# Chunked attention into a bilinear feed-forward: sums and scores in shared runs from block 4 on, and a last product in two column halves

## The chip, the cores and the metric

The kernel runs on one core of a Trainium2 chip. The metric is the device time of one execution in microseconds (us). The engines are TensorE (PE in the profile; PEld is its weight load), VectorE (DVE), ScalarE (ACT), GpSimd (POOL) and SyncE (SP), which here only issues DMAs.

## The reference

```
scores = q_c @ k_c^T / 8           # chunks of 64 tokens, 8 heads, head dim 64
attn   = exp(scores - max) / (sum + 1e-9)
x      = attn @ v                  # laid out as 4608 tokens x 512
out    = ((x @ w_a) * (x @ w_b)) @ w_out   # d_ff 1536, float32
```

The batch has 8 sequences of 576 tokens, so 4608 tokens in all.

## The kernel before

**Units and blocks.** Tokens go in 18 units of 256 (attention) and 9 blocks of 512 (feed-forward): block K uses units 2K and 2K+1. For a unit U there are these steps: `scores` (q times k in 64x64 tiles of TensorE, into two PSUM banks, then two exponentials on ScalarE into `E`), `sums` (E times a matrix of ones, also on 64x64 tiles, into two banks; two Ln on ScalarE, L305), `inverse` (exp of minus Ln, L314), and `values` (E times v on 64x64 tiles, then two multiplies on VectorE, L337, that write `xT`). Scores issued with `now=1` run the first exponential at once and keep the second in a list `late`, which `exps()` empties after `p5`.

**Loads.** `bring(U)` casts the unit's raw q and k on GpSimd (L213), loads unit U+1 on SP (L182), transposes q and k by DMA on SP (L248) and casts v.

**The feed-forward.** From block 2 on, d_ff goes in six groups of 256 (i = 0 to 5). Each group forms the two products of x with w_b and w_a by a seven-product scheme over 2x2 quarters: `p1` to `p7`, four matmuls each of 128x128 by 256 columns (L439). They accumulate in three banks: A (pool psum_a, "pa"), B (one of two banks "pb") and C (psum_c, "pc"). ScalarE copies A to B after `p1` (L457), and stages B after `p6` as u, A after `p2` as b, B after `p5` as v (L450). After `p7`, `add7` on VectorE makes c = C + v (L477) and C += u (L478); then `p3` adds to B and `p4` to C, each followed by a multiply into `ab_sb` (L489). Group i's `p3` and `p4` are issued inside group i+1. The buffers u, b, v, c have one copy each. GpSimd forms the sums of quarters of `ab_sb` (L519).

**The output.** `OutGroup(K-1)` does block K-1's product with w_out during block K, again with seven parts n = 0 to 6 in two halves th = 0, 1 of six matmuls (L575). Parts 0 and 1 go into A (psum_o, "po"), parts 2, 3 and 5 into B (psum_q, "pq"), parts 4 and 6 into C (psum_o again). After part 1 ScalarE writes half of o0 (L590); after 2 and 3 it stages u and v (L595, L598); after 5 it writes the rest of o0 (L602) and SP stores it. After part 4 VectorE writes half of o1 (L618) and does C += u (L622); after part 6 it writes the rest (L608) and SP stores it. At the very end, block 8's own output runs as two `OutGroup`s of one half each (`only` = 0, 1), on 256-column tiles.

**The order is written out by hand.** Each engine runs its instructions in the order of the program. `chunk(n)` takes the next n of the waiting halves of output parts; the table `chunks` holds two numbers for each group. `attend(K, i, n)` runs the attention steps that `at(...)` has put at that place. One group runs so:

```
now.p1()                 # and the copy A to B
if last: last.add7()
chunk(first number)
if last: last.p3()
attend(K, i, 0)
now.p6()
if last: last.p4(); finish(last)
now.p2()
chunk(second number)
attend(K, i, 1)
now.p5(); exps()
now.p7()
```

PSUM has eight banks: psum_a, two of psum_b, psum_c, psum_o, psum_q, and two of psum_t ("pt"). From block 2 on, sums and values take their banks from psum_t; scores take psum_o or psum_q, and the free one of psum_b.

Of the kernel before, what the change touches and what calls it, by code (L numbers as in the profile page):

```python
# [16 lines left out]
def kernel(  # L17
# [10 lines left out]
    nc = tc.nc  # L28
# [260 lines left out]

    def sums(U, halves=None):  # L290
        E = E_of[U]
        sm = [bank() for _ in range(2)]
        for cl in range(2):
            for j in range(2):
                nc.tensor.matmul(  # L295
                    sm[cl][j * 64:j * 64 + 64, :],
                    ones[cl * 64:cl * 64 + 64, :],
                    E[cl * 64:cl * 64 + 64, j].rearrange("p m g s -> p (m g s)"),
                    start=True,
                    stop=True,  # L300
                )
        ln_of[U] = sm_pool.tile([128, 2, NKT, 128], FP32, name="ln")
        rs_of[U] = ln_of[U]
        for cl in range(2):
            nc.scalar.activation(  # L305
                out=ln_of[U][:, cl].rearrange("p m n -> p (m n)"), in_=sm[cl], func=AF.Ln
            )
            if halves:
                inverse(U, cl)
# [8 lines left out]
    def values(U):  # L318
# [16 lines left out]
        for cl in range(2):  # L335
            x = x_tiles[K][:, :, 256 * u:256 * u + 256]
            nc.vector.tensor_tensor(  # L337
                out=x.rearrange("p m (g c s) -> p m g c s", g=2, c=2)[:, :, :, cl, :],
                in0=av[cl],
                in1=rs[:, cl].rearrange("p m (g s) -> p m g s", g=2),  # L340
                op=MULT,
            )

# [11 lines left out]

    def bring(U):

        if U >= NU:
            return
        cast(U, "qk")  # L360
        load(U + 1, "q" if U < 9 else "qkv")
        transpose_dma(U)
        bring_v(U)

# [160 lines left out]
    class OutGroup:  # L525
# [20 lines left out]
        def part(self, n, th):  # L546
# [26 lines left out]
            c0 = 0 if one else th * 256  # L573
            for kt in range(HFT):
                nc.tensor.matmul(  # L575
                    t[:, c0:c0 + 256],
                    a[:, kt, th * 128:th * 128 + 128],
                    w[:, kt],
                    start=n in (0, 4) and first and kt == 0,
                    stop=last and kt == HFT - 1,  # L580
                    skip_group_check=True,
                )
            if not last:
                return
# [22 lines left out]
            else:  # L607
# [4 lines left out]
                for c in [th] if one else range(2):  # L612
                    store(
                        self.K, 1, c, self.o1[:, c], lo if one else slice(0, DM),
                        nc.scalar if one and th else nc.sync,
                    )
            if n == (3 if one else 4):
# [35 lines left out]
    with tc.manual_schedule(  # L653
# [178 lines left out]
        def scores_beside(pool):  # L832
            return lambda u: scores(u, (pool, psum_b[0]), 1)

        for K in range(2, NBLK):
            U = 2 * K + 2
            if K == 2:
                at(K, 0, 0, lambda u: combine_x(2, (2, 3)), U)
                at(K, 0, 0, scores, U)
                at(K, 0, 1, sums, U)  # L840
            else:
                attention[K, 0, 0] = [lambda K=K: combine_x(K, (2,))]
                attention[K, 0, 1] = [lambda K=K: combine_x(K, (3,))]
                at(K, 0, 0, sums, U)
            at(K, 1, 0, inverse, U)
            at(K, 2, 1, values, U)
            at(K, 2, 1, scores_beside(psum_o), U + 1)
            at(K, 3, 0, sums, U + 1)
            at(K, 3, 1, inverse, U + 1)
            at(K, 4, 1, values, U + 1)  # L850
            at(K, 4, 1, scores_beside(psum_q), U + 2)
            at(K, 5, 0, lambda u: combine_x(u // 2, (0,)), U + 1)
            at(K, 5, 1, lambda u: combine_x(u // 2, (1,)), U + 1)

        def attend(K, i, n):
# [5 lines left out]
            2: (1, 1, 1, 1, 1, 2, 1, 2, 3, 0, 1, 1),  # L861
            4: (1, 1, 1, 1, 2, 1, 1, 2, 2, 0, 1, 1),
            NBLK - 1: (1,) * 12,
        }
# [8 lines left out]
        for K in range(2, NBLK):  # L873
            for i in range(NWP):
# [3 lines left out]
                if i == 1:  # L878
                    bring(2 * K + 4)
                elif i == 3 and K > 2:  # L880
                    bring(2 * K + 5)
                elif i == 3:
                    cast(9, "qk")
                    load(10)
                    transpose_dma(9)
                if i == 0:
                    g = OutGroup(K - 1)
                    outs += [
                        lambda g=g, n=n, th=th: g.part(n, th) for n in range(7) for th in range(2)
                    ]  # L890
                now = Group(K, i)
                now.p1()
                if last:
                    last.add7()
                chunk(chunks.get(K, chunks[4])[2 * i])
                if K == 2 and i == 0:
# [13 lines left out]
                now.p2()  # L910
                chunk(chunks.get(K, chunks[4])[2 * i + 1])
                attend(K, i, 1)
                now.p5()
                exps()
                now.p7()
                last = now
# [47 lines left out]
```

The softmax here doesn't subtract the row's maximum and nothing guards it: scores larger than these inputs give would overflow.

## Time and profile before

| | us |
|---|---|
| median of 11 runs | 303.9 (303.23 to 305.68) |
| the profiled execution | 303.88 |
| its span, first to last instruction | 302.1 |
| PE busy | 292.0 (97%) |
| DVE busy | 209.1 (69%) |
| ACT busy | 196.4 (65%) |
| POOL busy | 192.5 (64%) |

The granted TensorE clock is 1.0 over the span. A block of the steady part takes about 30 us: block 2 starts near 81, block 4 near 141, block 5 near 171, block 6 near 201. In the timeline one line merges instructions of one kind in order of time: its start, its length, the engine, the source line, the output and inputs by name, and the count.

### The profile page before, as it was taken

What the parts mean: (1) busy time and instruction counts of PE and PEld (TensorE: products, weight loads), DVE (VectorE), ACT (ScalarE), POOL (GpSimd) and SP (SyncE); (2) the same over time, 40 slices, a digit from 0 to 9 for tenths busy, and PEclk for the clock granted to TensorE, in tenths of its full rate; (3) what the DMA queues carried; (4) which work ended last, traced back from release to release, by engine and by line L of the source; (5) the groups of instructions that cost most, each with busy time, mean ns of one, the idle gap of its engine ahead of it and who ended that gap; (6) DMA issues with size and microseconds to landing.
All of it is one profiled execution on the core that took longest, in us unless ns stands there. A gap on an engine that the chain in (4) does not pass through costs nothing.

```text
span 302.1 us, 8588 instructions
## 1 busy us (share of the span) xinstructions
PE 292.0 (97%) x3519; PEld 231.6 (77%) x3521; DVE 209.1 (69%) x341; ACT 196.4 (65%) x355; POOL 192.5 (64%) x180
## 2 busy tenths in 40 slices
PE   6699999999999999999999999999999999999995
PEld 2344467866588888888888888888888888888884
DVE  3456576877757696769576967795779667965773
ACT  2743567448387769676867687768776877567532
POOL 0565758997699598908880888088817801790560
PEclk9999999999999999999999999999999999999999
DMA  7999999998999989989959495949731001100025
GB/s 225 304 374 289 282 342 351 239 219 201 202 246 270 183 201 271 229 189 242 213 114 229 148 211 121 224 152 207 112 99 72 2 2 69 72 1 3 2 79 199
DMA packets 140984, 54.29 MB, mean 180 GB/s; under 512 B 117137, under 2 KB 135057, under 8 KB 140945
## 3 DMA queue, kind: packets, MB, share of 16 engines
q1 hardware_dynamic: 140800, 53.62, 71.0%
q8 instruction: 27, 0.44, 0.6%
q10 hardware_dynamic: 144, 0.13, 0.1%
q14 instruction: 13, 0.10, 0.1%
HBM read 37.75 MB, written 9.44 MB: 156 GB/s over the span
## 4 chain that ended last, share of the span: by engine, by line
PE 83%; DMA 5%; SPq 4%; DVE 3%; POOL 1%; ACT 1%; issue 1%; DVEq 0%; ACTq 0%; POOLq 0%
PE pb L439 19%; PE pc L439 12%; PE pa L439 12%; PE po L575 12%; PE pq L575 10%; PE pb L643 3%; DMA st<-in_k_dram 3%; DMA st<-in_moe_w_b_dram 2%; PE po L389 2%; PE pc L389 2%; PE pa L389 2%; PE pq L389 2%; PE pt L295 2%; PE pt L328 2%; SPq L112 2%; SPq L194 1%
## 5 line engine op out<-in xcount | busy, mean ns | idle before, releaser
L519 POOL TENSOR_TENSOR so<-ab_sb 128x512 f16<-128x512 f16 x23 | 27.4, 1191 | 67.1 <-DVE ab_sb L489 67.1
L439 PEld LDWEIGHTS <-t 128*128 128x128 f16 x504 | 48.3, 98 | 8.5 <-issue 1.7
L439 PE MATMUL pb<-s,wa 128*128 128x256 f16 x336 | 50.6, 273 | 0.0
L439 PE MATMUL pa<-xT,wb 128*128 128x256 f16 x336 | 50.4, 273 | 0.0
L477 DVE TENSOR_TENSOR c_sb<-pc,v_sb 128x512 f32<-128x512 f32 x42 | 28.9, 689 | 28.7 <-ACT v_sb L450 28.7
L575 PEld LDWEIGHTS <-ab_sb 128*128 128x128 f16 x384 | 37.6, 98 | 4.7 <-issue 0.4
L439 PEld LDWEIGHTS <-wb 128*128 128x128 f16 x336 | 32.9, 98 | 4.0
L439 PEld LDWEIGHTS <-wa 128*128 128x128 f16 x336 | 31.8, 98 | 4.3 <-issue 0.2
L489 DVE SCALAR_TENSOR_TENSOR ab_sb<-pc,c_sb 128x512 f16<-128x512 f32 x42 | 29.0, 690 | 7.9 <-PE pc L439 6.7
L450 ACT COPY u_sb<-pb 128x512 f32<-128x512 f32 x42 | 24.7, 588 | 14.8 <-PE pb L439 14.7
L489 DVE SCALAR_TENSOR_TENSOR ab_sb<-pb,b_sb 128x512 f16<-128x512 f32 x42 | 29.0, 690 | 6.1 <-PE pb L439 5.2
L457 ACT COPY pb<-pa 128x512 f32<-128x512 f32 x42 | 24.1, 573 | 10.3 <-PE pa L439 10.0
L575 PEld LDWEIGHTS <-so 128*128 128x128 f16 x288 | 28.1, 98 | 3.4
L450 ACT COPY b_sb<-pa 128x512 f32<-128x512 f32 x42 | 25.0, 595 | 7.1 <-PE pa L439 7.1
L478 DVE TENSOR_TENSOR pc<-pc,u_sb 128x512 f32<-128x512 f32 x42 | 28.9, 689 | 0.0
L519 POOL TENSOR_TENSOR so<-so,ab_sb 128x512 f16<-128x512 f16 x23 | 27.0, 1174 | 1.7
L450 ACT COPY v_sb<-pb 128x512 f32<-128x512 f32 x42 | 24.6, 587 | 5.1 <-PE pb L439 4.4
L519 POOL TENSOR_TENSOR ab_sb<-ab_sb 128x512 f16<-128x512 f16 x23 | 26.7, 1162 | 0.0
L519 POOL TENSOR_TENSOR so<-ab_sb,so 128x512 f16<-128x512 f16 x23 | 26.1, 1162 | 0.0
L439 PE MATMUL pc<-xT,t 128*128 128x256 f16 x168 | 25.2, 273 | 0.1
L439 PE MATMUL pb<-s,t 128*128 128x256 f16 x168 | 25.3, 273 | 0.0
L439 PE MATMUL pc<-s,t 128*128 128x256 f16 x168 | 25.2, 273 | 0.0
(129 smaller groups left out, 565.8 us busy)
## 6 DMA issues: line engine op xcount, KB each, us to landing
out_dram<-o_sb SPq DMA_DIRECT2D x34, 256.0 KB, 2.3
st<-in_v_dram SPq DMA_DIRECT2D x32, 256.0 KB, 4.7
st<-in_k_dram SPq DMA_DIRECT2D x25, 256.0 KB, 4.8
st<-in_q_dram SPq DMA_DIRECT2D x23, 256.0 KB, 4.0
st<-in_moe_w_b_dram SPq DMA_DIRECT2D x6, 512.0 KB, 7.3
st<-in_moe_w_a_dram SPq DMA_DIRECT2D x6, 512.0 KB, 7.0
st<-in_moe_w_out_dram SPq DMA_DIRECT2D x6, 512.0 KB, 6.2
st<-in_q_dram SPq DMA_DIRECT2D x4, 512.0 KB, 5.6
```

The costliest lines, as they stand in the source:

```text
L112: nc.sync.dma_start(out=staged[n, i], in_=src[:, i * WCOL:i * WCOL + WCOL].rearrange("(kt r) c -> r kt c", r=128),)
L295: nc.tensor.matmul(sm[cl][j * 64:j * 64 + 64, :], ones[cl * 64:cl * 64 + 64, :], E[cl * 64:cl * 64 + 64, j].rearrange("p m g s -> p (m g s)"),
L389: nc.tensor.matmul(ps[n], w_ab[n, i][:, kt, o:o + 128], xT[:, kt, c0:c1], start=(kt == 0), stop=(kt == NKT - 1),)
L439: nc.tensor.matmul(t[:, h * 256:h * 256 + 256], w[:, kt, h * 128:h * 128 + 128], x[:, kt], start=start and h == 0 and kt == 0, stop=h == 1 ...
L450: nc.scalar.copy(out=t, in_=src)
L457: nc.scalar.copy(out=self.B, in_=self.A)
L477: nc.vector.tensor_tensor(out=self.c, in0=self.C, in1=self.v, op=ADD)
L478: nc.vector.tensor_tensor(out=self.C, in0=self.C, in1=self.u, op=ADD)
L489: nc.vector.scalar_tensor_tensor(out=self.dst[:, :, c0:c0 + 256], in0=t.rearrange("p (h n) -> p h n", h=2), scalar=AB_SCALE, in1=o.rearran ...
L519: (eng or nc.gpsimd).tensor_tensor(out=o, in0=x0, in1=x1, op=op)
L575: nc.tensor.matmul(t[:, c0:c0 + 256], a[:, kt, th * 128:th * 128 + 128], w[:, kt], start=n in (0, 4) and first and kt == 0, stop=last and ...
L643: nc.tensor.matmul(out_ps[K, tg], ab_tiles[K][:, ft, tg * 128:tg * 128 + 128], wo_sb[:, ft], start=(ft == 0), stop=(ft == NFT - 1),)
```

## The change

The last product (part 6 of the second half, at the very end) is done in two column halves of 128, each followed by its own VectorE operation and its own store, the first from SP's queue, the second from ScalarE's. Unit 1's last multiply into `xT` is done in two halves.

From block 4 on, three steps of different units share one run on 64x64 tiles: the values of a unit, the scores of the unit two on, and the sums of the next. The sums take psum_a and either psum_o or psum_q; the scores take psum_c and the free bank of psum_b. One of the two Ln is issued at once, the other waits in a list `late_ln` for the next `p1`. In block 4's first group the sums of unit 10 and the scores of unit 11 share a run. The output parts of blocks 4 to 7 run in the order 0, 1, 2, 3, 5, 4, 6, and `chunks` can hold a third number, for a chunk between `p5` and `p7`. From block 3's end on, the loads, casts and transposes of a unit are issued earlier: q and k of unit 2K+5 at group 1, its v at group 3, unit 2K+6 at group 5.

```diff
--- before.py
+++ after.py
@@ -287,9 +287,11 @@
             late.pop(0)()
             n -= 1
 
-    def sums(U, halves=None):
+    late_ln = []
+
+    def sums(U, halves=None, pools=(None, None)):
         E = E_of[U]
-        sm = [bank() for _ in range(2)]
+        sm = [bank(p) for p in pools]
         for cl in range(2):
             for j in range(2):
                 nc.tensor.matmul(
@@ -301,10 +303,15 @@
                 )
         ln_of[U] = sm_pool.tile([128, 2, NKT, 128], FP32, name="ln")
         rs_of[U] = ln_of[U]
+        ln = ln_of[U]
         for cl in range(2):
-            nc.scalar.activation(
-                out=ln_of[U][:, cl].rearrange("p m n -> p (m n)"), in_=sm[cl], func=AF.Ln
+            late_ln.append(
+                lambda cl=cl: nc.scalar.activation(
+                    out=ln[:, cl].rearrange("p m n -> p (m n)"), in_=sm[cl], func=AF.Ln
+                )
             )
+        for cl in range(1 if pools[0] else 2):
+            late_ln.pop(0)()
             if halves:
                 inverse(U, cl)
 
@@ -334,12 +341,13 @@
                         )
         for cl in range(2):
             x = x_tiles[K][:, :, 256 * u:256 * u + 256]
-            nc.vector.tensor_tensor(
-                out=x.rearrange("p m (g c s) -> p m g c s", g=2, c=2)[:, :, :, cl, :],
-                in0=av[cl],
-                in1=rs[:, cl].rearrange("p m (g s) -> p m g s", g=2),
-                op=MULT,
-            )
+            for m in (slice(0, 2), slice(2, 4)) if (U, cl) == (1, 1) else [slice(0, 4)]:
+                nc.vector.tensor_tensor(
+                    out=x.rearrange("p m (g c s) -> p m g c s", g=2, c=2)[:, m, :, cl, :],
+                    in0=av[cl][:, m],
+                    in1=rs[:, cl, m].rearrange("p m (g s) -> p m g s", g=2),
+                    op=MULT,
+                )
 
     def slot(s=None, f=None):
 
@@ -353,14 +361,15 @@
         if f is not None:
             values(f)
 
-    def bring(U):
+    def bring(U, names="qkv"):
 
         if U >= NU:
             return
         cast(U, "qk")
         load(U + 1, "q" if U < 9 else "qkv")
         transpose_dma(U)
-        bring_v(U)
+        if "v" in names:
+            bring_v(U)
 
     def bring_v(U):
         cast(U, "v")
@@ -571,16 +580,26 @@
                 lambda: (self.C, a22, t4),
             )[n]()
             c0 = 0 if one else th * 256
-            for kt in range(HFT):
-                nc.tensor.matmul(
-                    t[:, c0:c0 + 256],
-                    a[:, kt, th * 128:th * 128 + 128],
-                    w[:, kt],
-                    start=n in (0, 4) and first and kt == 0,
-                    stop=last and kt == HFT - 1,
-                    skip_group_check=True,
-                )
-            if not last:
+            end = n == 6 and one and th == 1
+            for cols in (slice(0, 128), slice(128, 256)) if end else [slice(0, 256)]:
+                for kt in range(HFT):
+                    nc.tensor.matmul(
+                        t[:, c0:c0 + 256][:, cols],
+                        a[:, kt, th * 128:th * 128 + 128],
+                        w[:, kt, cols],
+                        start=n in (0, 4) and first and kt == 0,
+                        stop=last and kt == HFT - 1,
+                        skip_group_check=True,
+                    )
+                if end:
+                    nc.vector.tensor_scalar(
+                        out=rows(self.o1, cols), in0=self.C[:, cols], scalar1=OUT_SCALE,
+                        scalar2=None, op0=MULT,
+                    )
+                    store(
+                        self.K, 1, th, self.o1[:, th], cols, nc.scalar if cols.start else nc.sync
+                    )
+            if not last or end:
                 return
             if n == 0:
                 self.B = self.bank(1)
@@ -610,10 +629,7 @@
                     scalar2=None, op0=MULT,
                 )
                 for c in [th] if one else range(2):
-                    store(
-                        self.K, 1, c, self.o1[:, c], lo if one else slice(0, DM),
-                        nc.scalar if one and th else nc.sync,
-                    )
+                    store(self.K, 1, c, self.o1[:, c], lo if one else slice(0, DM))
             if n == (3 if one else 4):
                 nc.vector.scalar_tensor_tensor(
                     out=rows(self.o1, hi), in0=halves(self.C), scalar=OUT_SCALE,
@@ -832,6 +848,9 @@
         def scores_beside(pool):
             return lambda u: scores(u, (pool, psum_b[0]), 1)
 
+        def sums_beside(pool):
+            return lambda u: sums(u, pools=(psum_a, pool))
+
         for K in range(2, NBLK):
             U = 2 * K + 2
             if K == 2:
@@ -841,14 +860,26 @@
             else:
                 attention[K, 0, 0] = [lambda K=K: combine_x(K, (2,))]
                 attention[K, 0, 1] = [lambda K=K: combine_x(K, (3,))]
-                at(K, 0, 0, sums, U)
-            at(K, 1, 0, inverse, U)
+                if K == 3:
+                    at(K, 0, 0, sums, U)
+            if K == 4:
+                at(K, 0, 1, sums, U)
+                at(K, 0, 1, scores_beside(psum_c), U + 1)
+            at(K, 1, 1 if K == 4 else 0, inverse, U)
             at(K, 2, 1, values, U)
-            at(K, 2, 1, scores_beside(psum_o), U + 1)
-            at(K, 3, 0, sums, U + 1)
+            if K < 4:
+                at(K, 2, 1, scores_beside(psum_o), U + 1)
+                at(K, 3, 0, sums, U + 1)
+            else:
+                at(K, 2, 1, scores_beside(psum_c), U + 2)
+                at(K, 2, 1, sums_beside(psum_o), U + 1)
             at(K, 3, 1, inverse, U + 1)
             at(K, 4, 1, values, U + 1)
-            at(K, 4, 1, scores_beside(psum_q), U + 2)
+            if K < 4:
+                at(K, 4, 1, scores_beside(psum_q), U + 2)
+            else:
+                at(K, 4, 1, scores_beside(psum_c), U + 3)
+                at(K, 4, 1, sums_beside(psum_q), U + 2)
             at(K, 5, 0, lambda u: combine_x(u // 2, (0,)), U + 1)
             at(K, 5, 1, lambda u: combine_x(u // 2, (1,)), U + 1)
 
@@ -859,8 +890,10 @@
         last = None
         chunks = {
             2: (1, 1, 1, 1, 1, 2, 1, 2, 3, 0, 1, 1),
-            4: (1, 1, 1, 1, 2, 1, 1, 2, 2, 0, 1, 1),
-            NBLK - 1: (1,) * 12,
+            3: (1, 1, 1, 1, 2, 1, 1, 2, 2, 0, 1, 1),
+            4: (0, 1, 1, (1, 1), 1, (1, 1), 1, 1, 1, (1, 1), 0, 1),
+            5: (1, 1, 1, (1, 1), 1, (1, 1), 1, 1, 1, (1, 1), 0, 1),
+            NBLK - 1: (1, 1, 1, (1, 1)) + (1,) * 8,
         }
 
         def finish(g):
@@ -876,23 +909,29 @@
                     for j in range(3):
                         combine_ab(K - 1, 3, j)
                 if i == 1:
-                    bring(2 * K + 4)
-                elif i == 3 and K > 2:
-                    bring(2 * K + 5)
+                    bring(2 * K + 4 if K < 4 else 2 * K + 5, "qkv" if K < 4 else "qk")
+                elif i == 3 and K == 3:
+                    bring(11)
                 elif i == 3:
-                    cast(9, "qk")
-                    load(10)
-                    transpose_dma(9)
+                    bring(9, "qk") if K == 2 else cast(2 * K + 5, "v")
+                elif i == 5 and K > 2:
+                    bring(2 * K + 6)
                 if i == 0:
                     g = OutGroup(K - 1)
                     outs += [
-                        lambda g=g, n=n, th=th: g.part(n, th) for n in range(7) for th in range(2)
+                        lambda g=g, n=n, th=th: g.part(n, th)
+                        for n in (range(7) if K < 4 else (0, 1, 2, 3, 5, 4, 6))
+                        for th in range(2)
                     ]
+                steps = chunks.get(K, chunks[5])[2 * i:2 * i + 2]
+                c0, c1, c2 = steps[0], *(steps[1] if type(steps[1]) is tuple else (steps[1], 0))
                 now = Group(K, i)
                 now.p1()
+                while late_ln:
+                    late_ln.pop(0)()
                 if last:
                     last.add7()
-                chunk(chunks.get(K, chunks[4])[2 * i])
+                chunk(c0)
                 if K == 2 and i == 0:
                     for j in range(3):
                         combine_wo(3, j)
@@ -908,10 +947,11 @@
                 if K == 2 and i == 4:
                     cast(9, "v")
                 now.p2()
-                chunk(chunks.get(K, chunks[4])[2 * i + 1])
+                chunk(c1)
                 attend(K, i, 1)
                 now.p5()
                 exps()
+                chunk(c2)
                 now.p7()
                 last = now
         ends = [
```

## The prediction

> **What bounds the kernel now.** I read the page's busy rows first, then TensorE's timeline over a block of the steady part, then the other engines beside it.
>
> ```profile
> span 302.1 us, 8588 instructions
> ...
> PE 292.0 (97%) x3519; PEld 231.6 (77%) x3521; DVE 209.1 (69%) x341; ACT 196.4 (65%) x355; POOL 192.5 (64%) x180
> ...
> L477 DVE TENSOR_TENSOR c_sb<-pc,v_sb 128x512 f32<-128x512 f32 x42 | 28.9, 689 | 28.7 <-ACT v_sb L450 28.7
> ```
>
> PE is busy all through. The windows answer gives PE 30.00 busy in each 30 us from 112 to 262, the blocks that the change touches: no engine makes PE wait there, so PE work removed is time gained, and every new PE wait is time lost in full. PE's timeline in block 6 (start, us, line, output<-inputs, count), from group 3's second product on:
>
> ```profile
> 217.27 0.60 PE L439 MATMUL pb<-s,wa 128*128 128x256 f16 x4
> 217.80 0.41 PE L295 MATMUL pt<-E,ones 64*64 64x512 bf16 x4
> 218.14 0.61 PE L439 MATMUL pb<-s,t 128*128 128x256 f16 x4
> 218.59 0.60 PE L439 MATMUL pc<-xT,t 128*128 128x256 f16 x4
> 219.03 0.60 PE L439 MATMUL pa<-xT,wb 128*128 128x256 f16 x4
> 219.46 1.48 PE L575 MATMUL po<-wot,ab_sb 128*128 128x256 f16 x12
> 220.77 0.60 PE L439 MATMUL pb<-s,wa 128*128 128x256 f16 x4
> ...
> 224.27 0.60 PE L439 MATMUL pc<-xT,t 128*128 128x256 f16 x4
> ```
>
> Starts tell more than durations: a product (L439, four matmuls) costs 0.44 (218.59 to 219.03), one half part of the output (L575, six) 0.655. The lone run of sums (L295) starts 0.09 late after the 217.27 product, and the next products come 0.34 and 0.45 on. 217.27 to 218.59 is 1.32; less two products, 0.88, the sums cost 0.45.
>
> VectorE beside it: the two operations of output part 4, the two adds of `add7`, then a multiply.
>
> ```profile
> 221.03 0.69 DVE L618 SCALAR_TENSOR_TENSOR o_sb<-po,vo_sb 128x512 f32<-128x512 f32 x1 [1.11 <-PE po L575]
> 221.76 0.70 DVE L622 TENSOR_TENSOR po<-po,uo_sb 128x512 f32<-128x512 f32 x1
> 222.37 0.68 DVE L477 TENSOR_TENSOR c_sb<-pc,v_sb 128x512 f32<-128x512 f32 x1
> 222.96 0.69 DVE L478 TENSOR_TENSOR pc<-pc,u_sb 128x512 f32<-128x512 f32 x1
> 224.03 0.69 DVE L489 SCALAR_TENSOR_TENSOR ab_sb<-pb,b_sb 128x512 f16<-128x512 f32 x1 [0.38 <-PE pb L439]
> ```
>
> The reader is to see that these four run without a gap from 221.03 to 223.65, 2.62 us, and that the `p4` product which needs the last (pc, 224.27) comes 0.6 later: covered now, but not by much. ScalarE copies A to B after each `p1`:
>
> ```profile
> 206.66 0.57 ACT L457 COPY pb<-pa 128x512 f32<-128x512 f32 x1 [0.24 <-PE pa L439]
> ```
>
> That `p1` started at 206.02, so B is ready 1.21 after `p1` starts; `p6`, which adds to B, started at 207.55 because an output part and `p3` lie between.
>
> **What the Trainium skill says.** TensorEngine Tiling (Array Packing), Tiling Modes, Key Properties: changing the tiling mode, not merely the tile, drains TensorE. The trace agrees: 0.09 into the run of 64x64 tiles, about 0.14 out. Perfetto Trace Analysis, Tensor Engine Instruction: a matmul's end is estimated, and VectorE and ScalarE keep strict order while TensorE may only pull weight loads ahead. The trace agrees: 0.60 shown for a product that the next follows after 0.44, and VectorE in the written order above. So a wait of one matmul holds all later ones, and a late add holds all later adds.
>
> **Part by part.**
>
> *Fewer runs of 64.* Blocks 4 to 7 now have eight lone sums runs and eight values or values-with-scores runs, 16. After: sums and scores in one at block 4's group 0, then two runs in each block, 9. Seven runs go, each with a switch in and a switch out. The sums themselves stay: four 512-column matmuls on four separate quarters stream once, 512 columns at 0.109 per 256, 0.22. 0.45 − 0.22 = 0.23 each, **−1.6**. Bounds: 0 (switching between values and 512-column sums inside a run costs as much) to 0.45 (the sums hide wholly).
>
> *Output parts after the change.* From block 5 the order by group is: 6b (of the block before), 0a / 0b, 1a, 1b / 2a, 2b, 3a / 3b, 5a / 5b, 4a, 4b / none, 6a. Here a and b are the two halves. So 4b stands in group 4 after `p5`, and group 5 has nothing between `p1` and `p3`. This is the step I hold decisive. L618 starts 0.91 after 4b's first matmul (its half of the x12 starts at 220.12, L618 at 221.03); L618, L622, L477, L478 take 2.62; a product follows an add by 0.04 (in the chain of waits, L478 ends at 87.32 and its product starts at 87.36). So `p4` of group 5 cannot start before 4b + 3.57. PE has 4b 0.655, `p7`, `p1`, `p3`, `p6` 0.437 each: 2.40. **PE stalls 1.17**, in each of blocks 4 to 7: **+4.7**. Now there are 4.15 between 4b and that `p4` (220.12 to 224.27). The attention multiplies don't add to this: they end 1.8 after the run starts, L618 can start at 2.3. Behind the stalled `p4` on PE stand `p2`, 6a and all else. Late next is ScalarE's copy of u (it needs the same L478), which `p5` wants 1.5 later: covered.
>
> *The copy A to B.* With nothing between, `p6` would start 0.87 after `p1`; B is ready at 1.21, plus 0.04: 0.38. In group 5 it lies inside the 1.17 (the adds end later), so counted once: block 4's group 0, whose first chunk is also empty: **+0.4**.
>
> *Block 4's group 0, sums and scores together.* Two Ln come ahead of the first exponential on ScalarE, and `p7` needs the scores' bank pc back. Sums start at run + 0.09, Ln 0.44 later (202.83 to 203.27), the operation after two Ln starts 0.97 after the first (204.24) and an exponential takes 0.60: run + 2.1. PE reaches `p7` at 0.70 for the run and 0.45 for `p5`, run + 1.15. **+1.0**, once. In the later runs the exponential comes first, ends by run + 1.5, and `p7` comes at 2.07: no cost. Sums into pa wait for the copy of b (over by run + 0.15, wanted at 0.6), and the next `p1` for Ln on pa (run + 2.0, wanted at 2.5): no cost, but without these covers 0.3 to 0.5 each.
>
> *inverse in group 3 behind one output half instead of two.* It takes 1.06 (0.96 to the next operation) between the copies of b and v: v comes 0.34 later, L478 ends 3.97 after `p2`, group 4's `p4` is due at 3.93: about 0.1, **+0.35** in four blocks; bounds 0 and 0.8.
>
> *Loads, casts, transposes.* Unit 2K+5's q and k are cast at group 1, v at group 3, unit 2K+6 at group 5. Each unit keeps three groups, about 13 us, from transposes to scores; transposes land in a median of 2.9 to 4.1 us. On POOL three casts (1.03 each) now stand ahead of the s-combines of groups 4 and 5. POOL was idle 7.8 us in every block before group 3's combine, so it is back in step by the fourth part. On SP the loads and transposes stand ahead of the o1 stores, whose tiles are wanted a block later. I cost all at nothing; without the POOL slack part 2 would wait up to 3 us per block.
>
> *Block 8 and the end.* Its part 4b moves to group 5. VectorE's L618 would start at 285.52 + 0.91 = 286.43 and the four end at 289.05, where L478 ends at 288.78 now; `p4` already waits for it there (288.83). **+0.27**, passed on through the chain at the end.
>
> *Last product in halves.* PE: 12 matmuls of 128 columns at 0.056 (eight 128x128 transposes took 0.45) for 6 of 256: the same 0.66. VectorE: 128x512 takes 0.69, 128x256 0.42, so 128 columns about 0.29: −0.13. But the first half's store is a sixth one on SP, whose last issue now ends near 299.23; it is issued to about 299.65, and lands no sooner than the single store from ScalarE's queue does (issued 299.50, median 1.8). The skill's DMA: Bandwidth & Descriptors, Anatomy of one DMA, has about 2 us fixed whatever the size; this trace's 128 KB stores, 1.7 and 1.8, fit that. I take **0**, bounds −0.15 and +0.3.
>
> *Unit 1's multiply.* xT's last multiply ends at 42.5 and PE waits 0.19 for it. Two halves of 0.42 free the first two matmuls 0.2 earlier: **−0.1**, bounds −0.2 and +0.1, since later waits may take it back.
>
> Sum: −1.6 + 4.7 + 0.4 + 1.0 + 0.35 + 0.27 + 0 − 0.1 = **+5.0**. The profiled execution took 303.88 (span 302.1 and 1.8 around it), and the median of the 11 runs is 303.9, so no shift: **308.8**.
>
> **Rivals.**
>
> 1. *Only the copy A to B binds*: VectorE catches up, for instance because fewer things stand before 4b than I list. −1.6, five waits of 0.38, 1.0 in block 4, −0.1: +1.2, 305.1. For it: VectorE is only 69% busy. Against: the four operations stood in an unbroken row in the trace.
> 2. *Faster*: the same place, group 5's `p4`. If 4b to the end of L478 is done in 2.40 rather than 3.57, and the copy in 0.87, no PE wait replaces the seven runs' switches: −1.7, 302.2. It decides where the stall is under 0.4 a block (0.4 × 4 = 1.6). Against: durations of L618 to L478 are fixed at 0.69 in every row. Equally, a switch pair would have to be worth 0.9.
> 3. *Merging saves nothing*, the stalls come: 310.4. Against: values to scores inside a run cost no visible gap.
>
> **How the numbers follow.** The forecast has 0.72, with an own range of 307.5 to 309.9 (inverse, covers, end); rival 1 0.13, rival 2 0.10, rival 3 0.05. The range 304.8 to 310.0 takes in rival 1 and the forecast's bounds. Faster by over 0.3% (0.9 us, about what a measurement of this kernel can tell from no change): 0.10; within: 0.05, rival 1 with smaller waits; slower: 0.85.
>
> **What would show it.** Right: in blocks 4 to 7, PE idle before `p4` of group 5 (pc<-xT,t) of about 0.8 after 0.4 before `p6`, put down to DVE pc L478 and ACT pb; nine L295/L328 runs; one wait of 1.0 for the exponential before `p7` in block 4; PE's starts otherwise in step. Wrong: PE unbroken through group 5, a wait at sums for pa or at part 2 for POOL, or scores waiting for transposes.

## The result, and the profile after

The changed kernel takes 311.06 us (median of 12, 309.68 to 313.56), the kernel before, run beside it, 304.06: ratio 1.024, 95% interval 1.021 to 1.026. That is slower by 7.0 where the forecast said 5.0. The profiled execution has a span of 309.1 us, 7.0 over that of before. (Line numbers from here on are those of the changed kernel: products L448, output halves L586, `add7` L486 and L487, multiply into `ab_sb` L498, copy A to B L466, the sum `s` of quarters of xT L428.)

The page of the profile after, where a group's last columns are busy us, mean ns, and idle time of the engine before it:

```profile
span 309.1 us, 8602 instructions
...
PE 294.2 (95%) x3525; PEld 232.3 (75%) x3527; DVE 211.7 (68%) x343; ACT 196.7 (64%) x355; POOL 193.8 (63%) x180
...
L448 PE MATMUL pc<-xT,t 128*128 128x256 f16 x168 | 25.2, 272 | 2.4 <-DVE pc L487 2.2
...
L448 PE MATMUL pb<-s,t 128*128 128x256 f16 x168 | 25.2, 273 | 1.3 <-ACT pb L466 1.3
L448 PE MATMUL pc<-s,t 128*128 128x256 f16 x168 | 25.2, 272 | 1.2 <-ACT E L279 0.8
```

PE fell from 97% busy to 95%. The three products named are `p4`, `p6` and `p7`; before, their idle columns were 0.1, 0.0 and 0.0. A list of TensorE's waits in blocks 4 to 7 up to 262 (what waited, for what; us in total, times, longest) says the same by cause:

```profile
PE pc L448 <- DVE pc L487: 1.6, 3, 0.5
PE pb L448 <- ACT pb L466: 1.1, 4, 0.3
PE pc L448 <- ACT E L279: 0.8, 1, 0.8
PE pc L448 <- DVE ab_sb L498: 0.3, 2, 0.2
```

The first three rows were forecast, the fourth was not. These columns count idle time from the modelled end of a matmul, which lies 0.16 after the next one could have started (0.60 shown for a product that costs 0.44). A wait below is therefore counted from start to start, less what the earlier instructions cost unhindered: 0.16 more each than shown. Group 5 of block 4, PE's timeline:

```profile
169.81 0.60 PE L448 MATMUL pb<-s,wa 128*128 128x256 f16 x4
170.69 0.60 PE L448 MATMUL pb<-s,t 128*128 128x256 f16 x4 [0.28 <-ACT pb L466]
171.81 0.60 PE L448 MATMUL pc<-xT,t 128*128 128x256 f16 x4 [0.53 <-DVE pc L487]
...
174.10 0.60 PE L448 MATMUL pc<-s,t 128*128 128x256 f16 x4 [0.16 <-DVE ab_sb L498]
```

VectorE's in the same stretch:

```profile
169.14 0.69 DVE L634 SCALAR_TENSOR_TENSOR o_sb<-po,vo_sb 128x512 f32<-128x512 f32 x1 [0.44 <-PE po L586]
169.87 0.70 DVE L638 TENSOR_TENSOR po<-po,uo_sb 128x512 f32<-128x512 f32 x1
170.47 0.68 DVE L486 TENSOR_TENSOR c_sb<-pc,v_sb 128x512 f32<-128x512 f32 x1
171.07 0.69 DVE L487 TENSOR_TENSOR pc<-pc,u_sb 128x512 f32<-128x512 f32 x1
171.67 0.68 DVE L498 SCALAR_TENSOR_TENSOR ab_sb<-pb,b_sb 128x512 f16<-128x512 f32 x1
172.27 1.18 DVE L428 TENSOR_TENSOR s<-xT 128x512 f16<-128x512 f16 x1
173.37 0.68 DVE L498 SCALAR_TENSOR_TENSOR ab_sb<-pc,c_sb 128x512 f16<-128x512 f32 x1
```

And GpSimd's:

```profile
170.17 1.03 POOL L213 CAST q_raw<-st 128x1024 bf16<-128x1024 f32 x1
171.15 1.03 POOL L213 CAST k_raw<-st 128x1024 bf16<-128x1024 f32 x1
172.13 1.03 POOL L213 CAST v_raw<-st 128x1024 bf16<-128x1024 f32 x1
```

And ScalarE's copy A to B:

```profile
170.07 0.57 ACT L466 COPY pb<-pa 128x512 f32<-128x512 f32 x1 [0.20 <-PE pa L448]
```

The copy ends at 170.64 and `p6` starts at 170.69; the forecast row L634 to L487 ends at 171.76 and `p4` starts at 171.81. So 0.44 is lost at `p6` and 0.69 at `p4`. Then a thing that was not forecast. `s` at L428 takes 1.18. It starts inside the cast of v (172.13 to 173.16) and ends 0.29 after it; the next such sum, at 173.97, starts while GpSimd is idle and takes 0.41. The multiply behind the slow one is late, it frees the bank that `p7` writes, and `p7` loses 0.32.

What the trace adds up to, from PE's starts:

| | forecast | in the trace |
|---|---|---|
| runs on 64x64 tiles, blocks 4 to 7 (16 before: 9.39; 9 after: 8.02) | −1.6 | −1.37 |
| group 5, `p6` (0.44 x3, 0.38) and `p4` (0.69 x3, 0.75) | +4.7 | +4.52 |
| block 4's group 0: `p6` 0.39, `p4` 0.11, `p7` 1.00 | +1.4 | +1.50 |
| group 4, `p4` (0.11 x4) | +0.35 | +0.44 |
| `p7` behind L498: 0.32 x2 in group 5, 0.21 x2 in group 0 | 0 | +1.06 |
| block 2, an output half waits for the w_out quarter sums (L164) | 0 | +0.76 |
| part 4 and `p4` of block 8, the end | +0.27 | +0.4 |

The last column sums to 7.3, for 7.0 of span: records of matmuls are missing here and there, and before had a wait of 0.05 in these blocks.

### The profile page after: what moved, and what is told of

Its sections match the earlier page's. It is cut to its first block, busy times and chain, and to the rows that moved or that the text cites. A ratio compares the mean times of both kernels' runs of the same rounds, so it can differ in the third digit from the quotient of the medians.

```text
span 309.1 us, 8602 instructions
## 1 busy us (share of the span) xinstructions
PE 294.2 (95%) x3525; PEld 232.3 (75%) x3527; DVE 211.7 (68%) x343; ACT 196.7 (64%) x355; POOL 193.8 (63%) x180
## 4 chain that ended last, share of the span: by engine, by line
PE 60%; DMA 17%; POOL 7%; DVE 6%; SPq 6%; issue 2%; ACT 1%; POOLq 0%; DVEq 0%
PE pb L448 15%; PE pc L448 11%; PE po L586 10%; PE pa L448 10%; PE pq L586 9%; DMA st<-in_k_dram 7%; DMA st<-in_moe_w_a_dram 5%; SPq L182 4%; DMA st<-in_moe_w_b_dram 2%; DMA st<-in_moe_w_out_dram 2%; DVE c_sb L486 2%; SPq L194 1%; DVE pc L487 1%; PE pt L335 1%; POOL so L528 1%
## 5 line engine op out<-in xcount | busy, mean ns | idle before, releaser
L448 PEld LDWEIGHTS <-t 128*128 128x128 f16 x504 | 48.8, 98 | 14.5 <-issue 8.2
L486 DVE TENSOR_TENSOR c_sb<-pc,v_sb 128x512 f32<-128x512 f32 x42 | 29.0, 690 | 39.0 <-ACT v_sb L459 25.5
L448 PE MATMUL pb<-s,wa 128*128 128x256 f16 x336 | 50.5, 273 | 0.0
L448 PE MATMUL pa<-xT,wb 128*128 128x256 f16 x336 | 50.4, 273 | 0.0
L586 PEld LDWEIGHTS <-ab_sb 128*128 128x128 f16 x390 | 37.8, 98 | 5.0 <-issue 0.7
L448 PEld LDWEIGHTS <-wa 128*128 128x128 f16 x336 | 31.7, 98 | 5.6 <-issue 1.8
L448 PEld LDWEIGHTS <-wb 128*128 128x128 f16 x336 | 32.9, 98 | 4.0
L498 DVE SCALAR_TENSOR_TENSOR ab_sb<-pc,c_sb 128x512 f16<-128x512 f32 x42 | 28.9, 689 | 5.4 <-PE pc L448 4.1
L466 ACT COPY pb<-pa 128x512 f32<-128x512 f32 x42 | 24.0, 573 | 13.3 <-PE pa L448 13.0
L498 DVE SCALAR_TENSOR_TENSOR ab_sb<-pb,b_sb 128x512 f16<-128x512 f32 x42 | 28.9, 687 | 4.5 <-PE pb L448 3.7
L586 PEld LDWEIGHTS <-so 128*128 128x128 f16 x288 | 28.1, 98 | 4.1 <-issue 0.6
L487 DVE TENSOR_TENSOR pc<-pc,u_sb 128x512 f32<-128x512 f32 x42 | 29.0, 690 | 0.0
L448 PE MATMUL pc<-xT,t 128*128 128x256 f16 x168 | 25.2, 272 | 2.4 <-DVE pc L487 2.2
L345 DVE TENSOR_TENSOR xT<-pt,ln 128x512 f16<-128x512 f32 x29 | 18.8, 686 | 12.4 <-PE pt L335 9.5
L448 PE MATMUL pb<-s,t 128*128 128x256 f16 x168 | 25.2, 273 | 1.3 <-ACT pb L466 1.3
L448 PE MATMUL pc<-s,t 128*128 128x256 f16 x168 | 25.2, 272 | 1.2 <-ACT E L279 0.8
```

The source lines that it names most:

```text
L345: nc.vector.tensor_tensor(out=x.rearrange("p m (g c s) -> p m g c s", g=2, c=2)[:, m, :, cl, :], in0=av[cl][:, m], in1=rs[:, cl, m].rearra ...
L448: nc.tensor.matmul(t[:, h * 256:h * 256 + 256], w[:, kt, h * 128:h * 128 + 128], x[:, kt], start=start and h == 0 and kt == 0, stop=h == 1 ...
L466: nc.scalar.copy(out=self.B, in_=self.A)
L486: nc.vector.tensor_tensor(out=self.c, in0=self.C, in1=self.v, op=ADD)
L487: nc.vector.tensor_tensor(out=self.C, in0=self.C, in1=self.u, op=ADD)
L498: nc.vector.scalar_tensor_tensor(out=self.dst[:, :, c0:c0 + 256], in0=t.rearrange("p (h n) -> p h n", h=2), scalar=AB_SCALE, in1=o.rearran ...
```

## The experiments

The theory: group 5's stall is VectorE's row after part 4b, with the copy A to B ahead of it, and a second, separate loss comes from the casts that now run beside VectorE's `s`. The rivals: the order of the output parts alone, the casts alone, or the run's order in block 4. Edits are against the changed kernel unless said otherwise.

**The row itself.** VectorE's second operation of part 4 is left out in blocks 4 to 7; a second kernel has the casts split as well (the edit of the casts stands further down).

```diff
-                nc.vector.tensor_tensor(out=self.C, in0=self.C, in1=self.u, op=ADD)
+                if one or not 3 <= self.K <= 6:
+                    nc.vector.tensor_tensor(out=self.C, in0=self.C, in1=self.u, op=ADD)
```

> Leaves out a part of the computation: VectorE's second operation after output part 4 (C += u, L638) in blocks 4 to 7; TensorE's work is unchanged. Theory (VectorE's unbroken row after part 4b sets p4 of group 5): the row is 0.60 shorter, so the wait before p4 of group 5 falls from 0.69 to about 0.1 in each of the four blocks, while the 0.44 before p6, which is ScalarE's copy A to B, stays. That is 2.4 us, and with the p7 waits of groups 5 and 0 (1.06 in all, VectorE's multiply comes 0.6 earlier) up to 3.0: a ratio to the kernel before of 1.013 to 1.016. Rival (what stalls p4 is p7's result or ScalarE's copy v, late as well, or the time comes back as a wait later in the block): the wait before p4 stays above 0.4, or new waits of 0.5 a block appear, and the ratio stays at 1.020 or more.

> The same operation left out in blocks 4 to 7, and the casts split as before (q and k of unit 2K+6 at group 3, its v at the next block's group 1). Theory (two separate causes, the row after part 4b and GpSimd's casts beside VectorE's s): both waits go, 2.4 and 1.06, so what is left in blocks 4 to 7 is 1.8 in group 5 before p6, 1.5 in block 4's group 0 and 0.4 in group 4, 3.7 to 4.1 in all, and the ratio is 1.010 to 1.014. Rival (one cause: with the row shorter, s no longer meets the casts): no difference to the run with the row alone, below 0.3 us.

Row alone: 308.08 us, ratio 1.012 (1.009 to 1.015), a little under the range expected. PE's timeline of that kernel, group 5 of block 4:

```profile
171.07 0.60 PE L448 MATMUL pb<-s,t 128*128 128x256 f16 x4 [0.28 <-ACT pb L466]
171.50 0.60 PE L448 MATMUL pc<-xT,t 128*128 128x256 f16 x4
```

`p4` follows `p6` after 0.43, with no wait, in all four blocks: 2.82 gone (L634 to L486 is 0.61 instead of 1.33). `p6` keeps its 0.44. Of the `p7` waits, those in group 5 went (0.64) and those in group 0, which were expected to go, grew from 0.21 to 0.45 twice: −2.98 with all three, beside the 3.0 expected at most. So the unbroken row sets `p4`. It does not set `p6`, which still starts just behind the copy A to B. They are two waits in series.

With the casts split too: 306.95, ratio 1.009 (1.006 to 1.012), 1.13 lower in the same comparison. The intervals of the two overlap; the trace separates them, no `p7` wait being left from block 4's group 1 to the end of block 7. Waits in blocks 4 to 7: 0.44 x3 and 0.39 in group 5, 0.11 x4 in group 4, 1.96 in block 4's group 0, together 4.11. So two causes, not one.

**Splitting the casts alone.** Unit 2K+6's q and k at group 3, its v at the next block's group 1, about as before the change.

```diff
+                    if K > 4:
+                        cast(2 * K + 4, "v")
...
-                    bring(9, "qk") if K == 2 else cast(2 * K + 5, "v")
-                elif i == 5 and K > 2:
-                    bring(2 * K + 6)
+                    if K == 2:
+                        bring(9, "qk")
+                    else:
+                        cast(2 * K + 5, "v")
+                        bring(2 * K + 6, "qk")
+                elif i == 5 and K == 3:
+                    bring(12)
```

> The changed kernel with one edit in blocks 4 to 6: the q and k of unit 2K+6 are loaded, cast and transposed at group 3 and its v is cast at the next block's group 1, so that no cast stands at group 5, where GpSimd's casts and VectorE's s lie side by side in the changed kernel. Theory (an add of two SBUF tensors on VectorE waits until GpSimd's running operation ends, and lateness of that s holds the multiply that p7 waits for): the s made in group 5 takes 0.4 to 0.6 and not 1.17, the p7 waits of 0.32 in group 5 go and the 0.21 in group 0 falls or stays; waits in blocks 4 to 7 fall from 7.5 to 6.3 to 6.9. Rival (as in e5_casts_later the wait only moves to the next s, because GpSimd has something to do there as well): within 0.4 of 7.5.

309.91, ratio 1.021 (1.019 to 1.023). VectorE's timeline in group 5 of block 4:

```profile
172.43 0.41 DVE L428 TENSOR_TENSOR s<-xT 128x512 f16<-128x512 f16 x1
173.37 0.41 DVE L428 TENSOR_TENSOR s<-s,xT 128x512 f16<-128x512 f16 x1
```

Both at 0.41, and all four `p7` waits gone; group 5's `p6` and `p4` and group 4's 0.11 are unchanged. The waits gone add up to 1.06, which is of the size of the run-to-run spread, so the total time alone would not have shown it.

**The same casts, a little later.** In group 5 they are issued after `p4`.

```diff
-                elif i == 5 and K > 2:
-                    bring(2 * K + 6)
...
+                if i == 5 and K > 2:
+                    bring(2 * K + 6)
```

> The changed kernel with one edit: the bring of unit 2K+6 in group 5 is issued after group 4's sums of quarters, not ahead of p1, so that GpSimd has no cast running while VectorE makes the first s of the next block. Theory (VectorE's add of 128x512 from SBUF takes 1.17 there because GpSimd runs at the same time): that add falls to 0.4 to 0.6 in blocks 4 to 6, and the 0.32 wait of p7 in group 5 goes (three times, about 1 us); the next group 0's 0.21 may stay or grow, since the casts now run beside its s. Rival (the add is long whatever GpSimd does): 1.17 and 0.32 stay.

310.02, ratio 1.021 (1.018 to 1.024). VectorE's timeline shows the loss move with the casts:

```profile
170.54 0.41 DVE L428 TENSOR_TENSOR s<-xT 128x512 f16<-128x512 f16 x1
...
175.27 1.24 DVE L428 TENSOR_TENSOR s<-xT 128x512 f16<-128x512 f16 x1
```

GpSimd's there:

```profile
175.19 1.04 POOL L213 CAST q_raw<-st 128x1024 bf16<-128x1024 f32 x1
```

In group 5 `s` is quick and `p7`'s 0.32 is gone. The `s` of the next group 0 now starts 0.08 behind a cast, ends 0.28 after it, and `p7` there loses 0.75. Where the casts run decides where VectorE loses.

**The output parts in the old order.** Parts 0 to 6, and an output half between `p1` and `p6` in every group (block 8's places are the old ones too); the second kernel spreads the halves over the groups differently.

```diff
-            4: (0, 1, 1, (1, 1), 1, (1, 1), 1, 1, 1, (1, 1), 0, 1),
-            5: (1, 1, 1, (1, 1), 1, (1, 1), 1, 1, 1, (1, 1), 0, 1),
+            5: (1, 1, 1, 1, 1, (1, 1), 2, 1, 1, 1, 1, 1),
...
-                        for n in (range(7) if K < 4 else (0, 1, 2, 3, 5, 4, 6))
+                        for n in range(7)
```

> The changed kernel with only the output parts' order and places put back near the old ones: order 0 to 6, in blocks 4 to 7 part 4b in group 3 and one part between p1 and p3 of every group. The shared runs on 64x64 tiles and the early loads stay. Theory (the place of part 4b and the empty chunks cost the time): the four waits of 1.13 at group 5 go, so do most of the p7 waits of groups 5 and 0 (1.06 together) and the 0.5 at block 4's group 0; new are up to 0.25 in each of three blocks where sums wait for bank pq. About 5 us faster than the changed kernel, near 306, about 1.006 of the kernel before. Rival (sharing the banks between sums, scores and products, or the early loads and casts, cost the time): the waits only move to other products, and it stays within 1.5 us of 311.

310.61, ratio 1.022 (1.020 to 1.025), as the rival had it. The two longest of TensorE's waits in its blocks 4 to 7, up to 262:

```profile
PE po L586 <- ACT ln L309: 2.2, 4, 0.6
PE pc L448 <- DVE pc L487: 1.1, 4, 0.3
...
```

The group 5 waits of `p6` and `p4` went, as the theory has it, and the time did not. Part 4a, at group 3, now needs the bank po, which the sums of the shared run hold until ScalarE's Ln: 0.74 x3 and 0.68. `add7` is late in group 0 instead (0.51 x2). The order 0, 1, 2, 3, 5, 4, 6 is the price of the sums' bank: with it the stall is in VectorE's row, without it in ScalarE's Ln.

The second such kernel keeps part 4a clear of that Ln:

```diff
-            at(K, 5, 0, lambda u: combine_x(u // 2, (0,)), U + 1)
+            at(K, 5, 1, lambda u: combine_x(u // 2, (0,)), U + 1)
...
+            4: (1, 1, 1, 1, 1, (1, 1), 1, 1, 2, 1, 1, 0),
+            5: (1, 1, 1, (1, 1), 1, (1, 1), 1, 1, 2, 1, 1, 0),
```

> The changed kernel with another placing: output parts in the order 0 to 6, part 4a after p2 of group 3 (not ahead of p3, where it waited 0.74 for the Ln on bank po in e1_parts), 4b and 5a together in group 4, one part between p1 and p3 in every group, and VectorE's first s of the next block moved from group 5's p3 to behind its p4. Theory (the waits come from where part 4's adds and that s stand on VectorE's queue, and from parts that ask for a bank that a shared run still holds): the 1.13 at group 5 goes without the 0.74 coming back, p7's waits fall under 0.2, block 4's group 0 loses 0.5 of its 1.5; 0.2 stays in each of three blocks where the sums wait for bank pq. About 5 us under the changed kernel, 305 to 306.5. Rival (the sharing of banks itself moves the waits about, wherever the parts stand): within 2 us of 311 again.

312.8, ratio 1.030 (1.027 to 1.033): worse, where 305 to 306.5 was expected. Both `s` now stand next to each other after the multiply in group 5, in the casts' time. PE's timeline in block 4's group 0, which loses 2.98 where the changed kernel lost 1.50:

```profile
144.29 0.61 PE L448 MATMUL pb<-s,t 128*128 128x256 f16 x4 [0.91 <-DVE s L428]
145.49 0.60 PE L448 MATMUL pc<-xT,t 128*128 128x256 f16 x4 [0.59 <-DVE pc L487]
149.33 0.60 PE L448 MATMUL pc<-s,t 128*128 128x256 f16 x4 [0.99 <-ACT E L279]
```

**Block 4's group 0.** Scores ahead of sums in the run.

```diff
-                at(K, 0, 1, sums, U)
                 at(K, 0, 1, scores_beside(psum_c), U + 1)
+                at(K, 0, 1, sums, U)
```

> The changed kernel with one edit: in block 4's group 0 the scores of unit 11 stand ahead of the sums of unit 10, so that the first exponential comes ahead of the two Ln. Theory (p7 waits for bank pc behind the two Ln): the 1.00 wait at p7 falls to 0.1 to 0.3, block 4 becomes 0.7 to 0.9 shorter, nothing else moves. Rival (the wait comes from the transposes of unit 11, which land late): the wait stays at about 1.0, or moves to the scores.

310.93, ratio 1.024 (1.021 to 1.027). `p7`'s wait for the exponential falls from 1.00 to 0.09, so the two Ln ahead of the exponential made that wait. But the two Ln, now behind the exponential, delay the copies of the next group, and `p6` of group 1 loses 0.60: 0.3 net, too little to see in the time.

**All of it together.** The second kernel's order of output parts, scores first with one Ln late, the second `inverse` at group 4, the last product whole; then the same with the casts split (and the move of `combine_x` from block 4 on only).

```diff
+                at(K, 0, 1, lambda u: sums(u, pools=(psum_t, psum_t)), U)
...
-            at(K, 3, 1, inverse, U + 1)
+            at(K, *((3, 1) if K < 4 else (4, 0)), inverse, U + 1)
```

> e7_parts_again, and three edits more: block 4's scores ahead of its sums, of which one Ln is put off to the next p1; inverse of group 3 moved to group 4, between p3 and p6; the last product whole with one store, as in the kernel before. Theory: blocks 4 to 7 have waits of about 1 us in all instead of 7.5, the shared runs keep their gain of 1.4, and the end is as before: 303 to 304.5, equal to the kernel before within 0.3% or up to 0.5% faster. Rival: the waits move again, and it stays over 306.

> e8_all with the casts of e10_casts_split, and with VectorE's first s moved behind p4 only from block 4's group 5 on. In e8_all blocks 4 to 7 still waited about 7.3: 1.08 and 0.46 in each block for VectorE's s with GpSimd's casts beside it, and 1.9 at block 4's group 0. Theory (what is left is VectorE behind GpSimd's casts): those fall to 0.2 to 0.5 in each block and to under 1 at block 4's group 0; waits of 2 to 3.5 in all, 304 to 306.5. Rival (VectorE's queue has too little room in groups 5 and 0, whoever runs beside it, once sums no longer stand between p3 and p6): the waits stay over 5, and it stays over 308.

310.73, ratio 1.023 (1.020 to 1.026), and with the casts split 307.65, ratio 1.013 (1.011 to 1.015); 303 to 304.5 and 304 to 306.5 were expected. The list of TensorE's waits of the latter from 139 to 262 has one row:

```profile
PE pc L448 <- DVE pc L487: 1.1, 4, 0.3
```

By starts 3.66 of wait are left in blocks 4 to 7, where the first had 7.28. Half of that is the split: `p7` in group 0 of blocks 5 and 6 loses 0.16 each instead of 1.08. The other half, 1.09 before `p6` and 0.76 before `p4` in block 4's group 0, and 0.59 more in block 3's group 0, lies where the split changes nothing: there the only difference is the place of `combine_x` in blocks 2 and 3. So the 3.1 between the medians is not the split's alone. The kernel still loses, since 1.37 saved by shared runs is less than 3.66; its profiled execution took 306.28 and was the fastest of five, 1.4 under the median, so the others lost more. No kernel here beat the one before.

**The ends.** Both stores after both halves of the last product:

```diff
-                if end:
-                    nc.vector.tensor_scalar(
...
+            for cols in (slice(0, 128), slice(128, 256)) if end else ():
+                nc.vector.tensor_scalar(
...
```

> The changed kernel with one edit at the very end: the last product still in two column halves of matmuls, but both VectorE operations and both stores come after the second half's matmuls. Theory (the second half's matmuls wait for VectorE's read of the first half, because both lie in one bank): the 0.49 gap inside the last product goes, and the last VectorE operation ends about 0.2 to 0.3 sooner than in the changed kernel. Rival (the gap comes from 128-column matmuls or their weight loads): the gap stays.

311.27, ratio 1.025 (1.023 to 1.028). PE's timeline of the changed kernel at the end:

```profile
304.82 0.50 PE L586 MATMUL pa<-wot,ab_sb 128*128 128x128 f16 x6
305.70 0.49 PE L586 MATMUL pa<-wot,ab_sb 128*128 128x128 f16 x6 [0.38 <-DVE o_sb L595]
```

And of this one:

```profile
305.34 0.83 PE L586 MATMUL pa<-wot,ab_sb 128*128 128x128 f16 x12
```

With the first half's VectorE operation between them, the second six matmuls start 0.88 after the first six, and without it 0.34: both halves lie in one bank, and TensorE waits 0.54 (not 0.49, as the expectation has it) until VectorE has read the first. From the last product's start to the issue of the last store it is 1.31 before, 1.74 after the change, 1.39 here; the total, of two executions, does not show these 0.35. The Trainium skill's PSUM — Partial Sum Buffer, PSUM bank collisions raise a hardware error, has it that two engines may not touch one bank in the same 32 partitions at once, disjoint columns or not, and that accesses are to be kept apart by bank. The trace agrees that they were kept apart here: the wait is for VectorE's read of other columns of the bank.

The two ends alone, on the kernel before (the edits of the last product and of unit 1's multiply, nothing else):

```diff
+            for m in (slice(0, 2), slice(2, 4)) if (U, cl) == (1, 1) else [slice(0, 4)]:
...
+            end = n == 6 and one and th == 1
```

> The kernel before with only the first two parts of the change: the last product in two column halves stored apart, and unit 1's last multiply in two halves. Theory (the second half waits for VectorE's read of the first in the same bank; what unit 1 gains is given back to a DMA wait): the last store is issued about 0.4 later after the last part's first matmul, a first product of block 0 starts 0.25 sooner and this is gone by 31 us; 0.2 to 0.5 us slower in all. Rival (these two parts gain what they aim at): 0.1 to 0.4 us faster.

304.17, ratio 1.0015 (1.0004 to 1.0026): +0.4 us. The same 0.54 stands before its second half.

## Why the prediction was right or wrong

**Output parts after the change: right.** 1.17 a block was forecast, 1.13 came (0.44 and 0.69), for the reason given: the row of four operations after part 4b, and the copy A to B inside the same stretch. Shortening the row removed the second wait and left the first. Rivals 1 and 2 needed VectorE to catch up; it did not. Rival 3's number, 310.4, lies nearest to the measured time, but by accident: its stalls came, and merging did save 1.37.

**Block 4's group 0: right.** 1.00 before `p7` and 0.39 before `p6`, for 1.0 and 0.4. Scores first took the 1.00 away.

**The inverse in group 3: right**, 0.44 for 0.35; what removed it is not shown apart from the other edits.

**Fewer runs of 64: mis-sized.** A shared run of values, scores and sums costs 1.02, values with scores 0.78, sums alone 0.44. A run saved is worth 0.196, not 0.23: the sums cost 0.25 inside a run where I took 0.22. Seven runs give 1.37.

**"Loads, casts, transposes: I cost all at nothing": the step that failed.** I asked only whether GpSimd would be back in step, and it was. I did not ask what its casts do to an engine that waits for nothing of theirs. The Trainium skill has it: SBUF — State Buffer, SBUF: two separate sides, says that VectorE with two SBUF inputs and GpSimd reading SBUF exclude each other for a whole instruction. The trace agrees: `s`, VectorE's one operation in these blocks that reads two SBUF tensors, took 0.41 alone and 1.18 to 1.24 behind a cast, ending about 0.3 after it, while VectorE's operations with an input in PSUM kept 0.68 to 0.70 beside the first two casts. It cost 1.06 in blocks 4 to 6: 0.64 in group 5 behind casts, and 0.42 in group 0, where `s` took 0.83 behind a sum of quarters on GpSimd. So casts are not special, and the trace of before already had the effect, here at the end of block 6, first GpSimd's sum and then VectorE's `s` (L419 there):

```profile
230.22 1.16 POOL L519 TENSOR_TENSOR so<-ab_sb 128x512 f16<-128x512 f16 x1 [1.04 <-DVE ab_sb L489]
```

```profile
231.09 0.57 DVE L419 TENSOR_TENSOR s<-s,xT 128x512 f16<-128x512 f16 x1
```

`s` takes 0.57 and ends 0.28 after GpSimd's sum. Only 0.29 of that sum was left to run, and TensorE lost nothing by it there. In block 6 and later no unit 2K+6 is left, no casts run in group 5, and the waits were gone there too.

**Block 2's 0.76** is not the change's: up to block 3's group 5 the program is the same but for unit 1's multiply, and no other profile has this wait. In this execution GpSimd waited for loads of w_out (1.54, 0.42, 0.24 and 1.00, between 46 and 53) and was 2.2 behind the kernel before at 53. It waited again for loads of k and v (2.92 and 0.68, up to 77.72), and its w_out sums ended at 96.95 instead of 94.46. Why those loads were late is not known.

Other profiles show a loss that this one lacks. Six profiles are of kernels with the same program at the end of block 3 and the start of block 4, where unit 12's casts now run. There `s` and the first cast start level, to within 0.01. In the changed kernel's own profile `s` at 139.85 took 0.42 and the cast 1.31, and in the profile of the kernel with scores first `s` won too. In the other four (the tail's, the split's, the two with the shorter row) `s` lost: in the split's, `s` at 139.07 took 1.31 and the cast 1.03. In these four `p7` of block 3's group 5 loses 0.33 to 0.38, and `p4` of block 4's group 0 0.64 instead of 0.11. So the changed kernel can lose 0.9 there as well; its profiled execution did not, and lost 0.76 in block 2 instead. The two losses are not tied to each other: the profile of the scores first has neither. The kernel before has such a place too, in block 2's group 5. In three profiles (the first with the old order of parts, the scores first, the shorter row) `s` there took 1.31 to 1.41, and `p7` lost 0.37 to 0.47.

**Last product in halves: outside the bounds of −0.15 to +0.3**, by little. I costed the matmuls, VectorE and the queues, and forgot the bank that both halves share: 0.54 of wait, 0.43 more to the last issue, +0.4 in the run of the ends alone. The stores came as forecast: halves of 64 KB took 1.9 and 1.6 us from issue to landing, where whole ones of 128 KB took 1.7 and 1.8.

**Unit 1's multiply: misplaced.** What I took at 42.5 is unit 2's, still whole. Unit 1's is at 17; the first product of block 0 starts at 17.56 instead of 17.82. By 30.3, where a transpose waits for a cast fed by DMA, the two traces are level again (30.32 and 30.35): 0.

**Block 8: 0 for 0.27.** `p4` waits 0.22 longer, and a later wait before part 4 fell from 0.38 to 0.15, so it was taken back.

The misses point one way: casts +1.06, block 2 +0.76, the end +0.4, runs +0.23, and +0.1 each for block 4's group 0, the inverse and unit 1, against −0.27 for block 8 and −0.18 in group 5: 2.3, which is the 7.3 of the table less 5.0. (The forecast's own sum, 303.9 and 5.0, is 308.9 and not the 308.8 written.)

## What to carry to other kernels

When a change moves work of an engine that nobody waits for, look at what its new neighbours share with it, not only at its slack: here a cast moved beside an addition of two SBUF tensors tripled that addition, and the addition stood ahead of what the full engine needed. When banks are borrowed to share a switch, write down who must give them back in the new order; each order tried here paid more for a bank or for an `add7` than the 0.2 us that a saved switch pair is worth. Two halves of a last step that lie in one PSUM bank did not overlap here: the second waited 0.54 us for the read of the first. Halves in different banks were not tried.

## What the runs showed of the hardware

VectorE's sums of two SBUF tensors and GpSimd's operations held each other up in both directions. In the thirteen profiles `s` (128x512, f16) starts 177 times inside a GpSimd operation that has 0.13 us or more left, 49 times in a cast and 128 times in a sum of quarters, and each time it ends 0.27 to 0.29 after that operation. It starts 168 times with nothing of GpSimd's in its way, and takes 0.41 to 0.42. In the remaining 19 both start within 0.02 of each other, and the tie goes either way: `s` won 10 of them and lost 9. At 139, losing it costs VectorE 0.90 us (1.31 for 0.41), and GpSimd 0.28 (1.31 for 1.03). VectorE's operations on 128x512 with an f32 input in PSUM showed nothing of it: 0.66 to 0.70, beside GpSimd's work or not.
